# Retention, two feed-forward stages and a soft mixture on one Trainium2 core: loads into the packs' places queued behind the last turning transfers, sums of the last softmax stage in two banks, second expert layer begun on half of its inputs

## The chip, the cores and the metric

The program runs on one core of a Trainium2 chip. The metric is the device time of one execution in microseconds (us). The core has five engines: PE (TensorE; its weight loads stand in the profile as PEld), ACT (ScalarE), DVE (VectorE), POOL (GpSimd) and SP (SyncE). In this kernel SP computes nothing: it is the queue from which every transfer (DMA) is issued, in program order.

## The reference: what is computed

The reference, cut to what matters:

```python
scores = scale * q @ k.T                       # 8 batches, 8 heads, 576 positions, 64 columns
ret = scores * Dmat                            # gamma_h ** (i - j) for i >= j, else 0
x = (ret @ v) as 4608 tokens x 512
h = x @ w_in                                   # 512 x 2048
x = (h * sigmoid(1.702 * h)) @ w_out           # 2048 x 512
logits = x @ phi                               # 512 x 32: 8 experts of 4 slots
d = softmax of logits over the tokens          # all 4608
slot_input = d.T @ x                           # 32 slots x 512
for e in range(8):
    slot_out[e] = max(slot_input[e] @ w1[e], 0) @ w2[e]      # 512 x 1024, 1024 x 512
c = softmax of logits over the slots
out = c @ slot_out
```

The second mixture needs the softmax over all tokens, so its experts can begin only when the last token has been through everything before.

## The kernel before, in words

The 4608 tokens are worked on in 12 blocks of 384 (`NB`, `NBLK`). For each block, PE forms the product with `w_in` in 16 pieces of 128 columns (`expert_scores`, L345, tile `hp`), ACT applies the gate (`gelu`, L355, tile `gT`), and the result has to be turned from columns-by-tokens to tokens-by-columns. For all blocks but the last, DVE turns 32 x 32 squares (`turn_fc`, L374, tile `pre`) and 16 transfers for each half of a block put the squares into their places (`shuffle`, L382, tile `nat`). These 32 transfers of a block are called the turning transfers here. In the last block (`n = LAST = 11`) PE does the turning itself (L369, tile `tpg`). The attention of a block (lines 193 to 259) is woven in between the pieces of the block before it; its operands lie in the tiles called packs.

The product with `w_out` is put off: the slots are linear in it, so `slots_part` (L449, tile `Sg`) multiplies the block's softmax weights with the turned gate output `nat`, one block late. For block 10 this happens in the last block after the seventh piece (`LAST_SLOTS_AT = 6`), in 12 products that appear as 24 rows in a trace (two passes each). The first two of them read the half of `nat` that was put in place first, the next two the second half.

The tail (`tail`, from L551) begins after the sixteenth piece of block 11: last logits, last softmax, `Sg` of block 11 (L602), the turning of the sums `acc` (L627), the product of the sums with `w_out` (L634, `si_ps`, one bank of PSUM, read out half by ACT at L638 and half by DVE at L639), the sum over the four column groups (L642), the first expert layer (L657, `h_ps`: 8 experts x 2 halves of 512 hidden columns), its turning (L665 to L676: two copies `hs`, 8 products `hT_ps` into one bank, a maximum with 0 into the zeroed tiles `hT`), the second expert layer in four quarters `q` of the 512 output columns (`second_layer`, L685, `so_ps`; each quarter reads 8 weight tiles), and for each quarter the sum over column groups (`slot_results`, L695) and the combination with `cT` (`result`, L710), whose five pieces are copied by ACT and DVE into tiles `ob` (L711) and written out (L712). Pieces of quarter `q - 1` stand between the experts of quarter `q`.

**The loads.** The tail needs 72 weight tiles of 128 x 1024 numbers of 4 bytes (512 KB each): 8 of the joined `w_out`, 32 of `w1`, 32 of `w2`. They are issued in the fixed order `todo` by `prefetch` (L480 to L498). Each takes the next *place*: a tile whose earlier content is done with. The places become free in the order of the program: a part of a buffer called `ring` and the buffer `raw`, the two `pre` buffers (3 each), 8 tiles of a pool `pw2` over the memory of the attention's packs (L765 to L767, opened in block 10 after its fourteenth piece), 3 views of the block's `x` (L776), the sixteen `w_in` tiles one after the other as block 11 finishes with them (L788), 4 tiles `pw3` over the memory of the gate (L586 to L588; beside them the pool holds two `hT` tiles and `hs`, 3 more tiles of the same size), 5 tiles `pt` (L616 to L618), and from then on the places of tiles that have been used in the tail (8 at L652, 4 after each expert at L660).

A load waits on SP until its place is free, and everything behind it on SP waits too. Each transfer also waits until the transfer issued eight before it has landed, so that at most eight are under way. The output is written in 20 pieces from SP as well, behind the last load.

Queue in block 10 around the change, as the loop of L730 to L767 issues it: the first 16 turning transfers of the block (after its tenth piece), 3 loads into `pre` (after the twelfth), 8 loads into `pw2` (after the fourteenth), the last 16 turning transfers (after the sixteenth).

Of the kernel before, what the change touches and what calls it, by code (L numbers as in the profile page):

```python
# [20 lines left out]
DM = H * D  # L21
DFF = 2048
NS = 32
NE = 8
SE = 4
EF = 1024
# [7 lines left out]
NFC = DFF // 128  # L34
# [5 lines left out]
NW3, NW4 = 4, 5  # L40
NQ = 4
# [88 lines left out]
def tile_kernel(ctx, tc, qkv, w_in, w_turned, w_out, phi, w1, w2, consts, out):  # L130
# [346 lines left out]
    def place_in(pool_, tag, bufs):  # L477
        return lambda: pool_.tile([128, 1024], F32, tag=tag, name="wx", bufs=bufs)
# [72 lines left out]
    def tail():  # L551
# [15 lines left out]
        act.copy(Lp[0:NS, 1], lt[0:NS])  # L567
# [7 lines left out]
        dve.reduce_max(mb, lt, axis=AX.X)  # L575
        dve.tensor_tensor(mnew, mb, st["m"], op=ALU.max)
# [9 lines left out]
        pw3 = ctx.enter_context(tc.tile_pool(name="pw3", bufs=NW3, side="right", reuse_waits="tile"))  # L586
# [4 lines left out]
        for t in hT_flat:  # L591
            pool.memset(t, 0.0)
# [24 lines left out]
        for _ in range(NW4):  # L617
            prefetch(place_in(pt, "w", NW4))  # L618
        ST = pt.tile([128, 4, 4, NS], F32, tag="s", name="ST", bufs=2)
# [10 lines left out]
        si_ps = ps.tile([128, DM], F32, tag="r", name="si_ps", bufs=3)  # L630
        for fl in range(4):
            for b in range(4):
                fc = 4 * b + fl
                pe.matmul(si_ps[32 * b:32 * b + 32, :], ST[:, fl, b, :], wx[0, fc // 2][:, fc % 2, :],  # L634
                          start=(fl == 0), stop=(fl == 3))
        combine_rest(NPRE, NTILE)
        dve.transpose(cT, Lall)
        act.activation(si4[:, 0:256], si_ps[:, 0:256], AF.Copy, scale=ssum)  # L638
        dve.tensor_scalar(si4[:, 256:512], si_ps[:, 256:512], ssum, None, op0=ALU.mult)  # L639
        sit_ps = ps.tile([128, NDC, NS], F32, tag="L", name="sit_ps")  # L640
        for dc in range(NDC):
            pe.matmul(sit_ps[:, dc, :], si4[:, dc * 128:(dc + 1) * 128], sum4[:, 0:NS], start=True, stop=True)  # L642
# [7 lines left out]
        dve.tensor_copy(own_slots(si_flat, 0, NE, NDC), sit_ps.rearrange("p c (e j) -> p e c j", j=SE))  # L650
# [4 lines left out]
        for e, hf in [(e, hf) for e in range(NE - 2) for hf in range(2)] + [(e, hf) for hf in range(2) for e in (NE - 2, NE - 1)]:  # L655
# [4 lines left out]
            if hf and e < NE - 2:  # L660
                for _ in range(NDC):
                    prefetch()

        hT = [t.rearrange("p (e c s) -> p e c s", c=EF // 128, s=NS) for t in hT_flat]
        act.copy(hs[:, 0], h_ps[0])  # L665
        act.copy(hs[:, 1, 0:256], h_ps[1][:, 0:256])
        dve.tensor_copy(hs[:, 1, 256:512], h_ps[1][:, 256:512])
        hT_ps = ps.tile([128, EF // 128, NS], F32, tag="L", name="hT_ps")
        for f in range(EF // 128):
            pe.matmul(hT_ps[:, f, :], hs[:, f // 4, (f % 4) * 128:(f % 4 + 1) * 128], sum4[:, 0:NS], start=True, stop=True)  # L670
        hv = hT_ps.rearrange("p c (e j) -> p e c j", j=SE)
        for i, k in ((0, 0), (0, 4), (1, 0), (1, 4)):
            c = slice(k, k + 4)
            dve.tensor_scalar(own_slots(hT_flat[i], 16 * i, 3, EF // 128)[:, :, c], hv[:, 4 * i:4 * i + 3, c], 0.0, None,
                              op0=ALU.max)
            dve.tensor_scalar(hT[i][:, 3, c, 16 * i + 12:16 * i + 16], hv[:, 4 * i + 3, c], 0.0, None, op0=ALU.max)  # L676
# [3 lines left out]
        def second_layer(q, e):  # L680
            if e == 0:
                SR[q] = ps.tile([128, DQ], F32, tag=("St", "L")[q % 2], name="so_ps")
            for f in range(EF // 128):
# [15 lines left out]
        homes = [(pw3, NW3)] * NW3 + [(pt, NW4)] * NW4  # L699

        def result(q, k):

            nt = min(8, NTILE - 8 * k)
            own, m = homes.pop(0)
            homes.append((own, m))
            ob = own.tile([128, 1024], F32, tag="w", name="ob", bufs=m)[:, 0:128 * nt]
            ov = ob.rearrange("p (t b i) -> p t b i", b=4, i=32)
            for b in range(4):
                op_ = ps.tile([128, 8, 32], F32, tag=("h", "r")[b % 2], name="op", bufs=3)[:, 0:nt]
                pe.matmul(op_, SR[q][32 * b:32 * b + 32], cT[32 * b:32 * b + 32, 8 * k:8 * k + nt, :], start=True, stop=True)  # L710
                (act.copy if b % 2 == 0 else dve.tensor_copy)(ov[:, :, b, :], op_)  # L711
            sp.dma_start(out[q, :, 1024 * k:1024 * k + 128 * nt], ob)  # L712

        NG = (NTILE + 7) // 8
        for q in range(NQ):
# [8 lines left out]
        for k in range(NG):  # L724
            result(NQ - 1, k)
# [107 lines left out]
```

## Time and profile before

| | |
|---|---|
| median of 3 runs | 683.14 us (681.36 to 685.93) |
| the profiled execution's own time | 682.53 us |
| its span, first to last instruction | 680.7 us |
| PE busy | 647.0 us, 95% of the span |
| DVE, ACT, POOL busy | 44%, 32%, 12% |
| moved by transfers | 150.67 MB, 221 GB/s over the span |
| output transfers | 16 of 512 KB and 4 of 256 KB |

Rows of the timeline give the start in us from the span's start, the time, the engine, the source line and the operation; in brackets stands how long the engine was idle before and what ended it. A row can merge several instructions (`x20`). SPq is SP as a queue: its time is issue time, not the transfer's. In rows by stretch, each engine's busy time stands with its number of instructions, then the granted clock of TensorE as a share of 2.4 GHz, the mean busy share of the 16 DMA engines and what they moved.

### The profile page before, as it was taken

Reading aid. Unit: us, or ns where it says so; the run is one execution under the profiler, and the core shown is the slowest. Engines: PE = TensorE matmul, PEld = TensorE weight load, DVE = VectorE, ACT = ScalarE, POOL = GpSimd, SP = SyncE. Lnnn points to the kernel's source line nnn. Section 1 sums busy time; section 2 is a strip of 40 time slices with the busy share of each in tenths; the row PEclk is TensorE's granted clock in tenths of the full one; section 3 lists DMA queues with packets and bytes.
Section 4 is the critical chain, followed back from the end, with each engine's and each line's share of the span. In section 5 each row is a group of like instructions: output and inputs, shape, how many; then the busy total and the mean of one; then the engine's idle time right before and its main releaser. Section 6 shows DMA issues by size and latency. Waiting matters only on the chain.

```text
span 680.7 us, 19516 instructions
## 1 busy us (share of the span) xinstructions
PE 647.0 (95%) x8595; PEld 550.0 (81%) x8595; DVE 297.3 (44%) x594; ACT 220.6 (32%) x429; POOL 80.2 (12%) x72
## 2 busy tenths in 40 slices
PE   8699999899999999999999999999999996998994
PEld 8697788688997988989989979899899894863663
DVE  3799824334453462454444533534544331222143
ACT  1675332132241242232422412423324141230143
POOL 1102102111101102021011011111110000010000
PEclk9799999999999999999999999999999999999998
DMA  7989465586776747646747567476477388989998
GB/s 277 392 291 336 161 156 147 133 191 210 198 251 152 194 138 196 178 156 193 186 123 199 162 153 203 148 186 180 149 198 200 68 289 234 410 290 370 408 409 339
DMA packets 67732, 150.67 MB, mean 221 GB/s; under 512 B 8768, under 2 KB 42944, under 8 KB 63040
## 3 DMA queue, kind: packets, MB, share of 16 engines
q1 hardware_dynamic: 67648, 149.43, 69.6%
q8 instruction: 67, 1.10, 0.7%
q14 instruction: 17, 0.14, 0.1%
HBM read 101.16 MB, written 13.63 MB: 169 GB/s over the span
## 4 chain that ended last, share of the span: by engine, by line
PE 72%; DMA 16%; SPq 5%; DVE 4%; ACT 1%; issue 1%; ACTq 0%
PE hp L345 48%; DMA wx<-in_moe_w_dram 6%; PE Sg L449 5%; PE Lg L389 4%; SPq L382 4%; DMA pack<-in_qkv_dram 4%; PE Sp L216 4%; PE St L216 3%; PE Op L216 2%; DMA early_raw<-in_moe_w_in_dram 2%; DMA out_dram<-ob 2%; DMA nat<-pre 1%; PE op L710 1%; PE warm L515 1%; DMA wx<-wo_dram 1%
## 5 line engine op out<-in xcount | busy, mean ns | idle before, releaser
L345 PE MATMUL hp<-x,w 128*128 128x384 f32 x2304 | 423.9, 341 | 3.1 <-ACT x L241 2.6
L345 PEld LDWEIGHTS hp<-x,w 128*128 128x128 f32 x2304 | 399.4, 189 | 30.4 <-issue 21.5
L374 DVE STREAM_TRANSPOSE pre<-gT 128x384 f32<-128x384 f32 x172 | 96.9, 572 | 185.8 <-ACT gT L355 159.6
L355 ACT ACTIVATE gT<-hp 128x384 f32<-128x384 f32 x188 | 91.4, 489 | 235.2 <-PE hp L345 235.1
L246 POOL TENSOR_TENSOR x<-xs,x 128x512 fp32r<-128x512 f32 x33 | 42.7, 1293 | 301.4 <-ACT x L241 301.4
L216 PE MATMUL Op<-pack 64*64 64x64 f32 x2176 | 72.2, 220 | 3.0 <-issue 2.4
L216 PEld LDWEIGHTS Op<-pack 64*64 64x64 f32 x2176 | 66.8, 135 | 3.6 <-issue 2.8
L222 POOL TENSOR_TENSOR pack<-pack,cs 128x512 f32<-128x512 f32 x32 | 34.5, 1080 | 170.3 <-DMA pack<-in_qkv_dram 129.2
L241 ACT CAST x<-xs 128x512 fp32r<-128x512 f32 x36 | 22.3, 620 | 87.6 <-DVE xs L234 87.6
L216 PE MATMUL Sp<-pack 64*64 64x64 f32 x1152 | 41.1, 222 | 3.3 <-DMA pack<-in_qkv_dram 3.3
L216 PEld LDWEIGHTS Sp<-pack 64*64 64x64 f32 x1152 | 37.7, 138 | 4.9 <-issue 2.6
L216 PEld LDWEIGHTS St<-pack 64*64 64x64 f32 x1024 | 33.2, 137 | 8.1 <-issue 8.1
L389 PE MATMUL Lg<-gT,Wp 128*32 128x384 f32 x376 | 38.5, 496 | 1.2 <-DVE Wp L322 0.7
L449 PE MATMUL Sg<-nat,dn 128*32 128x512 f32 x264 | 33.8, 617 | 5.3 <-DMA nat<-pre 5.3
L226 DVE TENSOR_TENSOR pack<-Sp,cs 128x512 f32<-128x512 f32 x36 | 24.8, 689 | 30.7 <-PE Op L216 19.8
L216 PE MATMUL St<-pack 64*64 64x64 f32 x1024 | 37.5, 224 | 0.1
L449 PEld LDWEIGHTS Sg<-nat,dn 128*32 128x32 f32 x264 | 9.4, 113 | 24.7 <-issue 24.6
L234 DVE TENSOR_TENSOR xs<-Op,cs 128x512 f32<-128x512 f32 x36 | 24.5, 680 | 4.4 <-PE Op L216 4.4
L290 ACT ACTIVATE early_raw<-early_raw 128x512 f32<-128x512 f32 x28 | 19.2, 690 | 18.0 <-DMA early_raw<-in_w_turned_dram 9.1
L230 DVE TENSOR_TENSOR pack<-St,cs 128x512 f32<-128x512 f32 x32 | 21.7, 680 | 4.6 <-PE St L216 3.4
L455 DVE SCALAR_TENSOR_TENSOR acc<-acc,corr,Sg 128x512 f32<-128x512 f32 x10 | 7.5, 748 | 36.2 <-PE Sg L449 36.2
L711 DVE COPY ob<-op 128x256 f32<-128x256 f32 (+1 forms) x40 | 14.0, 393 | 21.1 <-PE op L710 16.4
(127 smaller groups left out, 390.7 us busy)
## 6 DMA issues: line engine op xcount, KB each, us to landing
pack<-in_qkv_dram SPq DMA_DIRECT2D x36, 1024.0 KB, 5.6
nat<-pre SPq DMA_DIRECT2D x352, 96.0 KB, 2.2
wx<-in_moe_w_dram SPq DMA_DIRECT2D x60, 512.0 KB, 8.6
raw<-in_moe_w_out_dram SPq DMA_DIRECT2D x16, 512.0 KB, 4.8
out_dram<-ob SPq DMA_DIRECT2D x16, 512.0 KB, 9.2
early_raw<-in_moe_w_in_dram SPq DMA_DIRECT2D x14, 512.0 KB, 9.6
early_raw<-in_w_turned_dram SPq DMA_DIRECT2D x14, 512.0 KB, 6.8
wo_dram<-ring SPq DMA_DIRECT2D x16, 256.0 KB, 2.0
```

The costliest lines, as they stand in the source:

```text
L216: pe.matmul(o[oh, p, j, :], w[h, a, p, j], w[h, b, p, j], start=first_, stop=True, skip_group_check=True)
L222: pool.tensor_tensor(k, k, by_state(ksc[:, n % NPB, :]), op=ALU.mult)
L226: dve.tensor_tensor(packs[n][:, SC], Sps.pop(n), across(dtab), op=ALU.mult)
L234: dve.tensor_tensor(xss[g], Ops.pop(g), across(osc), op=ALU.mult)
L241: act.copy(xh[b_][:, :, i * CP:(i + 1) * CP], xss[g].rearrange("p a j c -> p a (j c)"))
L246: (eng or pool).tensor_tensor(xl[b_][:, :, cols_], xss.pop(g).rearrange("p a j c -> p a (j c)"), xh[b_][:, :, cols_], op=ALU.subtract)
L345: pe.matmul(hp, wt[fc][:, a, dc, :], b[n][:, dc, :], start=(i == 0), stop=(i == 3 * NDC - 1))
L355: act.activation(gT[n, g][:, fl, :], hps.pop((n, fc)), AF.Gelu_apprx_sigmoid)
L374: dve.transpose(pre[n, hf][:, :, :, fh, :].rearrange("p c b i -> p (c b) i"), gT[n, g][:, fl, :].rearrange("p (x j) -> p x j", j=32))
L382: sp.dma_start(nat[n][32 * b:32 * b + 32, :, a, hf * HF:(hf + 1) * HF, :], pre[n, hf][32 * a:32 * a + 32, :, b])
L389: pe.matmul(Lg[n][32 * fl:32 * fl + 32, :], Wp[:, g * GF + fl, :], gT[n, g][:, fl, :], start=(g == 0), stop=(g == NFC // GF - 1))
L449: pe.matmul(Sg[32 * b:32 * b + 32], dn[n][:, c, :], nv[:, 4 * b:4 * b + 4], start=(c == 0), stop=(c == NT128 - 1))
```

## The change

It has six parts.

1. The 8 loads into `pw2` are issued after block 10's sixteenth piece and behind `shuffle(n, 1)`, the last turning transfers, instead of in front of them.
2. `pw3` holds 7 places instead of 4. `hT` (2 tiles) and `hs` have no memory of their own any more: they take the first three places that the first layer's first expert leaves, and are zeroed then (POOL).
3. In the tail, DVE's maximum over `lt` stands ahead of ACT's copy of `lt` into `Lp` (they read one bank).
4. `si_ps` becomes two tiles of 256 columns in two banks (32 products of 256 columns for 16 of 512), both read out by ACT; `sit_ps` becomes two tiles; DVE's transposition of `cT` moves behind the copies into `siT`.
5. `hT_ps` becomes two tiles, a bank for each half of the hidden columns. The first half is turned while the second half of the last expert is still being formed, and quarter 0 of the second layer runs over all experts on inner columns 0 to 3 first, then on 4 to 7, with the turning of the second half after its fourth expert.
6. `result` forms two pieces at once (a whole bank for each `op` tile), after the fourth and sixth expert and one after the eighth; the 12 places `ob` go round among 7 + 5 instead of 4 + 5.

```diff
-NW3, NW4 = 4, 5
+NW3, NW4 = 7, 5
...
-        act.copy(Lp[0:NS, 1], lt[0:NS])
...
         dve.reduce_max(mb, lt, axis=AX.X)
+        act.copy(Lp[0:NS, 1], lt[0:NS])
...
-        for _ in range(NW3):
-            prefetch(place_in(pw3, "w", NW3))
-        hT_flat = [pw3.tile([128, 1024], F32, tag=f"hT{i}", name="hT", bufs=1) for i in range(2)]
-        hs = pw3.tile([128, 2, 512], F32, tag="hs", name="hs", bufs=1)
+        homes = [(pw3, f"w{i}", 1) for i in range(NW3)]
+        for i in (3, 4, 5, 6, 0, 1, 2):
+            prefetch(place_in(*homes[i]))
...
+        si_ps = [ps.tile([128, DM // 2], F32, tag="r", name="si_ps", bufs=3) for _ in range(2)]
+        for hf in range(2):
+            for fl in range(4):
+                for b in range(4):
+                    fc = 4 * b + fl
+                    pe.matmul(si_ps[hf][32 * b:32 * b + 32, :], ST[:, fl, b, :],
+                              wx[0, fc // 2][:, fc % 2, 256 * hf:256 * hf + 256], start=(fl == 0), stop=(fl == 3))
+        act.activation(si4[:, 0:256], si_ps[0], AF.Copy, scale=ssum)
+        act.activation(si4[:, 256:512], si_ps[1], AF.Copy, scale=ssum)
...
+        def turn_sums(i):
+            for f in range(4):
+                pe.matmul(hT_ps[i][:, f, :], hs[:, i, f * 128:(f + 1) * 128], sum4[:, 0:NS], start=True, stop=True)
...
+        for e in range(NE - 2):
+            for hf in range(2):
+                first_layer(e, hf)
+            if e == 0:
+                hT_flat = [places.pop(0)() for _ in range(2)]
+                hT = [t.rearrange("p (e c s) -> p e c s", c=EF // 128, s=NS) for t in hT_flat]
+                hs = places.pop(0)().rearrange("p (a f) -> p a f", a=2)
+                for t in hT_flat:
+                    pool.memset(t, 0.0)
+            for _ in range(1 if e == 0 else NDC):
+                prefetch()
+        first_layer(NE - 2, 0)
+        first_layer(NE - 1, 0)
         act.copy(hs[:, 0], h_ps[0])
...
+        first_layer(NE - 2, 1)
+        turn_sums(0)
+        first_layer(NE - 1, 1)
+        act.copy(hs[:, 1], h_ps[1])
...
+        for e in range(NE):
+            second_layer(0, e, range(0, 4))
+            if e == 3:
+                turn_sums(1)
+        for e in range(NE):
+            second_layer(0, e, range(4, 8))
+        sums_out(0)
+        for q in range(1, NQ):
             for e in range(NE):
                 second_layer(q, e)
-                if q and e == 1:
+                if e == 1:
                     slot_results(q - 1)
-                elif q and e > 2:
-                    result(q - 1, e - 3)
+                elif e in (3, 5, 7):
+                    result(q - 1, {3: (0, 1), 5: (2, 3), 7: (4,)}[e])
...
                     if fc == WINDOWS[-1]:
                         att_ctx.close()
                         pw2 = ctx.enter_context(tc.tile_pool(name="pw2", bufs=NW2, side="right", reuse_waits="tile"))
+                    if fc == NFC - 1:
                         for _ in range(NW2):
                             prefetch(place_in(pw2, "w", NW2))
```

Line numbers in the rows that follow, marked with - and +, are those of the kernel before and of the changed kernel. On SP, from the first half of block 10's turning transfers (`nat<-pre`) to the last load of a weight tile (`wx`, `ring`):

```order
 L382 DMA nat<-pre 32x3x256 x16
-L497 DMA wx<-wo_dram 128x1024 x6
-L497 DMA wx<-in_moe_w_dram 128x1024 x5
+L497 DMA wx<-wo_dram 128x1024 x3
 L382 DMA nat<-pre 32x3x256 x16
-L497 DMA wx<-in_moe_w_dram 128x1024 x31
+L497 DMA wx<-wo_dram 128x1024 x3
+L497 DMA wx<-in_moe_w_dram 128x1024 x39
 L497 DMA ring<-in_moe_w_dram 128x1024
-L497 DMA wx<-in_moe_w_dram 128x1024 x24
+L497 DMA wx<-in_moe_w_dram 128x1024 x21
```

Eleven loads stood ahead of the second 16 turning transfers, and three do now; behind them stand 64 instead of 56. Behind the load into `ring`, the first whose place the product with `w_out` leaves, 21 remain instead of 24.

On PE, from the last experts of the first layer (`h_ps`) to the first sum of quarter 0 (`sr_ps`), before:

```order
L657 MATMUL h_ps<-ring,siT 32x512 x3
L657 MATMUL h_ps<-wx,siT 32x512 x5
L657 MATMUL h_ps<-ring,siT 32x512 x3
L657 MATMUL h_ps<-wx,siT 32x512 x2
L670 MATMUL hT_ps<-sum4r,hs 128x32 x8
L685 MATMUL so_ps<-wx,hT 32x128 x56
L685 MATMUL so_ps<-ring,hT 32x128 x8
L685 MATMUL so_ps<-wx,hT 32x128 x16
L695 MATMUL sr_ps<-so_7516,sum4r 128x128
```

and now (the tiles `hs` and `hT` lie in places and are called `wx` here):

```order
L660 MATMUL h_ps<-wx,siT 32x512 x5
L660 MATMUL h_ps<-ring,siT 32x512
L666 MATMUL hT_ps<-sum4r,wx 128x32 x4
L660 MATMUL h_ps<-ring,siT 32x512 x2
L660 MATMUL h_ps<-wx,siT 32x512 x2
L701 MATMUL so_ps<-wx 32x128 x16
L666 MATMUL hT_ps<-sum4r,wx 128x32 x4
L701 MATMUL so_ps<-wx 32x128 x64
L711 MATMUL sr_ps<-so_7535,sum4r 128x128
```

The eight turning products stood together behind the last expert; four of them stand inside it now and four inside the second layer's quarter 0.

## Rows read from the trace of the kernel before

**Rows 1.** The page's head and its row of busy time.

```profile
span 680.7 us, 19516 instructions
PE 647.0 (95%) x8595; PEld 550.0 (81%) x8595; DVE 297.3 (44%) x594; ACT 220.6 (32%) x429; POOL 80.2 (12%) x72
```

**Rows 2.** Busy time by stretch, the last 130 us, core 0.

```profile
557.00:568.20 11.20, 10.70 (x67) 9.75 (x66) 5.16 (x12) 6.42 (x11) 0.00 (x0) 1.00 1.03 346
568.20:576.50 8.30, 2.99 (x15) 1.25 (x18) 0.00 (x0) 0.49 (x1) 0.00 (x0) 0.93 0.67 154
576.50:600.00 23.50, 23.50 (x152) 19.08 (x145) 3.53 (x6) 5.10 (x12) 0.00 (x0) 0.95 1.02 405
600.00:620.00 20.00, 17.48 (x126) 9.97 (x124) 7.77 (x21) 6.88 (x16) 2.82 (x3) 1.00 0.82 273
620.00:676.00 56.00, 48.51 (x824) 28.68 (x824) 15.61 (x50) 14.87 (x50) 0.00 (x0) 0.98 1.03 411
676.00:680.70 4.70, 0.00 (x0) 0.00 (x0) 0.00 (x0) 0.00 (x0) 0.00 (x0) 0.50 0.35 140
```

**Rows 3.** Timeline of PE, 563 to 582 us.

```profile
564.95 4.45 PE L345 MATMUL hp<-x,w 128*128 128x384 f32 x24
569.33 1.05 PE L449 MATMUL Sg<-nat,dn 128*32 128x512 f32 x4
575.69 4.24 PE L449 MATMUL Sg<-nat,dn 128*32 128x512 f32 x20 [5.31 <-DMA nat<-pre]
```

**Rows 4.** Timeline of SP, 540 us to the end: every transfer issued.

```profile
539.82 6.45 SPq L382 DMA_DIRECT2D nat<-pre  x10
548.91 2.73 SPq L497 DMA_DIRECT2D wx<-wo_dram  x6
551.68 4.92 SPq L497 DMA_DIRECT2D wx<-in_moe_w_dram  x5
557.60 16.39 SPq L382 DMA_DIRECT2D nat<-pre  x16
574.09 41.16 SPq L497 DMA_DIRECT2D wx<-in_moe_w_dram  x31
616.42 0.33 SPq L497 DMA_DIRECT2D ring<-in_moe_w_dram  x1
618.14 28.81 SPq L497 DMA_DIRECT2D wx<-in_moe_w_dram  x24
647.91 25.51 SPq L712 DMA_DIRECT2D out_dram<-ob  x20
```

**Rows 5.** Waits of SP, 500 us to the end: waited for, us in total, times, longest.

```profile
SPq L497 <- PE tpg L369: 12.9, 6, 2.7
SPq L497 <- PE hp L345: 6.3, 3, 2.7
SPq L827 <- DMA out_dram<-ob: 6.2, 1, 6.2
```

**Rows 6.** The line of the loads, L497: its transfers' time from issue to landing.

```profile
DMA to landing us min/median/max: 4.0/8.2/11.4
```

**Rows 7.** Timeline of DVE, 549 to 556 us: the last turning of block 10.

```profile
552.13 0.58 DVE L374 STREAM_TRANSPOSE pre<-gT 128x384 f32<-128x384 f32 x1 [1.50 <-ACT gT L355]
```

**Rows 8.** Timeline of the tail: `Sg`, quarter 0 of the second layer, the last copies.

```profile
610.15 2.78 PE L602 MATMUL Sg<-nat,dn 128*32 128x512 f32 x24 [0.35 <-DVE dn L597]
...
636.55 3.27 PE L685 MATMUL so_ps<-wx,hT 128*32 128x128 f32 x112 [0.30 <-DVE hT L674]
...
668.53 3.77 DVE L711 COPY ob<-op 128x256 f32<-128x256 f32 x10 [1.74 <-ACT SR L697]
```

**Rows 9.** Busy time by stretch, two stretches of 4 us, core 0.

```profile
552.00:556.00 4.00, 4.00 (x27) 3.12 (x26) 1.14 (x2) 1.07 (x3) 0.00 (x0) 1.00 0.94 351
576.00:580.00 4.00, 4.00 (x21) 0.95 (x14) 0.04 (x1) 0.00 (x0) 0.00 (x0) 0.66 0.99 369
```

More of the change, by code (lines that the diff above doesn't have):

```diff
@@ L585, in tail @@
         gate_ctx.close()
-        pw3 = ctx.enter_context(tc.tile_pool(name="pw3", bufs=NW3, side="right", reuse_waits="tile"))
-        for _ in range(NW3):
-            prefetch(place_in(pw3, "w", NW3))
-        hT_flat = [pw3.tile([128, 1024], F32, tag=f"hT{i}", name="hT", bufs=1) for i in range(2)]
-        hs = pw3.tile([128, 2, 512], F32, tag="hs", name="hs", bufs=1)
-        for t in hT_flat:
-            pool.memset(t, 0.0)
+        pw3 = ctx.enter_context(tc.tile_pool(name="pw3", bufs=1, side="right", reuse_waits="tile"))
+        homes = [(pw3, f"w{i}", 1) for i in range(NW3)]
+        for i in (3, 4, 5, 6, 0, 1, 2):
+            prefetch(place_in(*homes[i]))
         dp = ps.tile([128, NT128, 128], F32, tag="L", name="dp")
@@ L618, in tail @@
             prefetch(place_in(pt, "w", NW4))
+        homes += [(pt, "w", NW4)] * NW4
         ST = pt.tile([128, 4, 4, NS], F32, tag="s", name="ST", bufs=2)
@@ L629, in tail @@
         dve.tensor_copy(ST[:, 2:4].rearrange("p f b s -> p f (b s)"), tps[1])
[L630 to L635, printed above, removed]
+        si_ps = [ps.tile([128, DM // 2], F32, tag="r", name="si_ps", bufs=3) for _ in range(2)]
[7 more added lines that the diff above has]
+        act.activation(si4[:, 256:512], si_ps[1], AF.Copy, scale=ssum)
         combine_rest(NPRE, NTILE)
[L637 to L640, printed above, removed]
+        sit_ps = [ps.tile([128, 2, NS], F32, tag=t, name="sit_ps") for t in ("L", "St")]
         for dc in range(NDC):
-            pe.matmul(sit_ps[:, dc, :], si4[:, dc * 128:(dc + 1) * 128], sum4[:, 0:NS], start=True, stop=True)
+            pe.matmul(sit_ps[dc // 2][:, dc % 2, :], si4[:, dc * 128:(dc + 1) * 128], sum4[:, 0:NS], start=True, stop=True)
         def own_slots(t, s0, ne, n):
@@ L649, in tail @@
         siT = si_flat[:, 0:NE * NDC * NS].rearrange("p (e c s) -> p e c s", e=NE, s=NS)
-        dve.tensor_copy(own_slots(si_flat, 0, NE, NDC), sit_ps.rearrange("p c (e j) -> p e c j", j=SE))
+        for i in range(2):
+            dve.tensor_copy(own_slots(si_flat, 0, NE, NDC)[:, :, 2 * i:2 * i + 2],
+                            sit_ps[i].rearrange("p c (e j) -> p e c j", j=SE))
+        dve.transpose(cT, Lall)
         for _ in range(NFC // 2):
@@ L654, in tail, with first_layer @@
         h_ps = [ps.tile([128, 512], F32, tag="r", name="h_ps", bufs=3) for _ in range(2)]
-        for e, hf in [(e, hf) for e in range(NE - 2) for hf in range(2)] + [(e, hf) for hf in range(2) for e in (NE - 2, NE - 1)]:
+        hT_ps = [ps.tile([128, 4, NS], F32, tag=t, name="hT_ps") for t in ("L", "St")]
+        def first_layer(e, hf):
             for dc in range(NDC):
@@ L659, in tail @@
                           start=(e == 0), stop=(e == NE - 1))
[L660 to L664, printed above, removed]
-        act.copy(hs[:, 0], h_ps[0])
[L666 to L676, printed above, removed]
-        SR = {}
[L680 to L683, printed above, removed]
+        def turn_sums(i):
+            for f in range(4):
+                pe.matmul(hT_ps[i][:, f, :], hs[:, i, f * 128:(f + 1) * 128], sum4[:, 0:NS], start=True, stop=True)
+            hv = hT_ps[i].rearrange("p c (e j) -> p e c j", j=SE)
+            c = slice(4 * i, 4 * i + 4)
+            for k in range(2):
+                dve.tensor_scalar(own_slots(hT_flat[k], 16 * k, 3, EF // 128)[:, :, c], hv[:, 4 * k:4 * k + 3], 0.0, None,
+                                  op0=ALU.max)
+                dve.tensor_scalar(hT[k][:, 3, c, 16 * k + 12:16 * k + 16], hv[:, 4 * k + 3], 0.0, None, op0=ALU.max)
@@ new lines, in tail, with second_layer @@
+        first_layer(NE - 2, 0)
+        first_layer(NE - 1, 0)
+        act.copy(hs[:, 0], h_ps[0])
+        first_layer(NE - 2, 1)
+        turn_sums(0)
+        first_layer(NE - 1, 1)
+        act.copy(hs[:, 1], h_ps[1])
+        SR = {}
+        def second_layer(q, e, fs=range(EF // 128)):
+            if q not in SR:
+                SR[q] = ps.tile([128, DQ], F32, tag="r" if q == 0 else ("St", "L")[q % 2], name="so_ps",
+                                bufs=3 if q == 0 else 1)
+            for f in fs:
@@ L697, in slot_results @@
             act.copy(SR[q], sr_ps)
[L699 to L707, printed above, removed]
-            for b in range(4):
[L709 to L712, printed above, removed]
@@ L714, in tail, with result @@
-        NG = (NTILE + 7) // 8
-        for q in range(NQ):
+        def result(q, ks):
+            ops, nts = [], [min(8, NTILE - 8 * k) for k in ks]
+            for b in range(4):
+                ops.append(ps.tile([128, 2, 8, 32], F32, tag=("h", "r")[b % 2], name="op", bufs=3))
+            for i, k in enumerate(ks):
+                for b in range(4):
+                    pe.matmul(ops[b][:, i, 0:nts[i]], SR[q][32 * b:32 * b + 32],
+                              cT[32 * b:32 * b + 32, 8 * k:8 * k + nts[i], :], start=True, stop=True)
+            for i, k in enumerate(ks):
+                home = homes.pop(0)
+                homes.append(home)
+                ob = home[0].tile([128, 1024], F32, tag=home[1], name="ob", bufs=home[2])[:, 0:128 * nts[i]]
+                ov = ob.rearrange("p (t b i) -> p t b i", b=4, i=32)
+                for b in range(4):
+                    (act.copy if b % 2 == 0 else dve.tensor_copy)(ov[:, :, b, :], ops[b][:, i, 0:nts[i]])
+                sp.dma_start(out[q, :, 1024 * k:1024 * k + 128 * nts[i]], ob)
@@ L722, in tail @@
             sums_out(q)
         slot_results(NQ - 1)
-        for k in range(NG):
-            result(NQ - 1, k)
+        for k in range((NTILE + 7) // 8):
+            result(NQ - 1, (k,))
     with tc.manual_schedule(engines={getattr(mybir.EngineType, e) for e in ("PE", "Activation", "DVE", "Pool", "SP")}):
```

## The prediction

> **What bounds the kernel now.** I read the page's head first: PE is busy 95% of the span [rows 1]. That share is an average over the twelve blocks and says little about the end, where the whole change lies. So I next read the busy time by stretch, from 557 us on [rows 2]. From 576.5 to 600 us PE has no idle time and the transfers run at 405 GB/s with the DMA engines full. From 600 to 620 us the DMA share falls to 0.82 at 273 GB/s and PE is busy for 17.48 of 20 us. From 620 to 676 us the transfers run at 411 GB/s, without a break, while PE is idle for 7.5 of 56 us. So over the last 60 us the 16 DMA engines are the bound: the end comes when the last byte is out. The timeline of SP says the same at its end: the last of 20 output transfers has been issued at 647.91 + 25.51 = 673.4 us, and SP then waits 6.2 us for them to land [rows 4, 5], so the last lands at 679.6 us. The last copy on DVE ends at 668.53 + 3.77 = 672.3 us [rows 8], 7.3 us before that.
>
> Then I looked for idle time ahead of this stretch. PE: in 568.2 to 576.5 us it is busy for 2.99 of 8.3 us [rows 2]. The timeline of PE gives the place: four rows of Sg of block 10, an idle time of 5.31 us that the turning transfers end, then the other 20 rows in 4.24 us [rows 3]. In the tail 24 such rows take 2.78 us [rows 8], so 20 would take 2.32; the missing 1.9 us is the clock. The granted clock over 576 to 580 us is 0.66 [rows 9], part of the stretch at 1.2 instead of 2.4 GHz, after an idle PE. The stall thus costs PE 5.3 + 1.9 = 7.2 us. Transfers: between 600 and 620 us they move 273 where 411 would go, 20 x (1 - 273/411) = 6.7 us lost. The waits of SP say why: loads wait on PE's products and turnings, nine times, 19.2 us together [rows 5]. The queue runs dry because PE gives places back too late.
>
> **Calibrating the sum.** A unit is 512 KB, 524,288 bytes; at 405 to 411 GB/s it takes 1.295 to 1.276, say 1.285 us. The fastest load lands 4.0 us after its issue [rows 6], 2.7 more than its own unit. From 574.09 us on there are 31 + 1 + 24 = 56 loads [rows 4] and the output's 16 + 4/2 = 18 units: 74 x 1.285 = 95.1 us. If the engines were never idle, the last would land at 574.1 + 2.7 + 95.1 = 671.9. It lands at 679.6. Of the 7.7 us, 6.7 are the dry time above; the other 1.0 I take as the emptying of the 16 engines at the end, which stays.
>
> **The moved loads (part 1).** Now three loads stand ahead of the last 16 turning transfers instead of eleven. These transfers need DVE's last turning, which ends at 552.13 + 0.58 = 552.7 us [rows 7]. SP issues one in 6.45/10 = 0.645 us when nothing holds it [rows 4], 10.3 us for 16, so the last is out at 563.0. The wait for the transfer eight places before should not bite: three loads issued from 548.9 are 3.9 us of transfer and so land at about 555.5, and the sixth turning transfer, the first to wait for one of them, comes at 556. Before, PE started 575.69 - (557.60 + 16.39) = 1.7 us after the last issue [rows 3, 4]; so the half is in place at about 564.7. PE asks for it at 569.33 + 1.05 = 570.4 [rows 3]: 5.7 us of margin. The 5.31 us and the slow clock go, and all of PE behind it comes 7.2 us earlier.
>
> The price is that eight loads come later. The first of the 64 behind the turning transfers is issued at 563.0. By 574.1, when the first of 56 was issued before, (574.1 - 563.0)/1.285 = 8.6 units have gone through, against the 8 that were put behind. The stream is 0.6 unit, 0.8 us, ahead. No PE instruction between 563 and 606 us reads a loaded tile, so the delay itself stops nothing.
>
> **Three more places (part 2).** Of the loads, 21 instead of 24 remain behind the ring place. Three units, 3.9 us of transfer, can be issued earlier, when the gate's memory is free. That alone makes no byte fewer; it is a cushion for the stretch in which the queue ran dry. The memory of hT and hs now becomes free only after expert 0 and is zeroed then. The zeroing is POOL's, and its first reader comes six experts later: nothing.
>
> **The sum.** With places 7.2 us earlier, against 6.7 us of dry time, and three units of cushion, the queue should not run dry. Then 563.0 + 2.7 + (64 + 18) x 1.285 + 1.0 = 563.0 + 2.7 + 105.4 + 1.0 = 672.1 us for the last landing, 7.5 before 679.6 (0.8 + 6.7). At 1.276 and 1.295 us a unit it would be 671.3 and 672.9, and if the 1.0 us is not there, 671.1: the gain lies between 6.7 and 8.5.
>
> **Parts 3 to 6, PE's own chain.** PE's idle time in 600 to 620 us is 2.5 us [rows 2], and that is the most that the earlier maximum, the two banks of si_ps and the split of sit_ps can win there. Against it, 16 more products, 32 rows, stand in si_ps: at least 0, as the columns stay the same, and at most 32 x 3.27/112 = 0.93 us, the rate of the 128-column rows [rows 8], which I take as near 0 since 256 columns are the work. Turning inside the last expert can win the 0.30 us ahead of so_ps [rows 8] and perhaps as much again. So PE's last copy ends between 672.3 - 7.2 - 3.1 = 662.0 and 672.3 - 7.2 + 0.9 = 666.0. The last piece then needs 4.0 us or a little more to land alone, at most 670.5, still ahead of 672.1. I put these four parts at 0: the DMA stream covers them. If that cover were gone they would be worth what was just bounded. Pieces in pairs on 12 places ask nothing of the end, because output transfers already queue behind loads.
>
> So the profiled 682.53 would become 675.0. The median of the runs shown, 683.14, is 0.6 above that execution; on its scale I forecast 683.1 - 7.5 = 675.6 us.
>
> **A rate that speaks against it.** The sum needs 105 us at over 400 GB/s without a break. The rows have that for 80 us [rows 2], but not always: 351 GB/s at 552 to 556 and 369 at 576 to 580, both when a run of loads starts [rows 9]. The Trainium skill (SBUF — State Buffer, section "Summary: rules for kernel authors") says to reckon with about 358 GB/s between HBM and SBUF. By that a unit would be 1.46 us and the forecast 14.7 us later, 690.3, a slower kernel. The 411 GB/s over 56 us speak against the rule here, so I keep 1.285 and let the slow rate be a rival.
>
> **Rivals.**
> - *The queue still runs dry in part.* The turning transfers stay late, held by the three loads ahead of them (behind eleven loads the 16 took 16.39 us [rows 4]; at that pace the half would be in place at 570.8, 0.4 us after PE asks), or PE loses time elsewhere, with its clock low again. If PE gains 4 us instead of 7.2, dry time of about 2.7 us stays and the gain is 4.8: 678.3. For it: SP holds everything in order. Against it: the margin of 5.7 us.
> - *The move does not remove the wait.* PE finds another late input at Sg, or waits as long elsewhere before the places are given back. Then only the 0.8 us of the stream stays: 682.3. Against it: the other input, the block's softmax weights, was ready, since the first four rows ran.
> - *Slower: the stream's rate.* Place: the 82 units from 563 us on. Before, 11 loads went out while PE still had products to do and a dry stretch followed, so a low rate at the start of a run cost nothing; now every unit counts at the end. Break-even is 7.5/82 = 0.09 us more a unit, 381 GB/s. At 369 the end is 11.2 us later than forecast: 686.8. At 351 it is 17.1 us later: 692.7. For it: the two rows at the start of runs. Against it: 405 and 411 in long runs.
>
> **How the numbers follow.** About 1% is what a measurement of this kernel can tell from no change; faster by that is below 676.3, slower above 690.0. Forecast 0.69, with a range of its own of 673.5 to 678.5: three quarters of it, 0.53, below 676.3, the rest, 0.16, within 1%. Dry in part 0.18, wait not removed 0.08, both within 1%. Slow rate 0.05, counted as slower. So faster 0.53, same 0.42, slower 0.05. The range of 8 in 10 reaches from 672.0, the best of the sum with a median 2 us low, to 682.0, which takes in the partly dry queue and leaves out most of the last two cases.
>
> **What would show it.** Right: no idle time of PE of over 1 us at Sg of block 10, its 24 rows in about 2.8 us, no fall of the granted clock at 575 us, over 400 GB/s in every stretch from 566 us to the end, and the last landing near 672. Wrong: SP waiting on PE for places with the DMA share under 0.95 between 590 and 615 us (dry in part), Sg still waiting for turning transfers, or a stream below 385 GB/s. If DMA is idle near the end and PE is not, PE's chain was the bound and parts 3 to 6 mattered.

## The result and the profile after

The changed kernel takes 673.56 us (median of 4 runs, 671.62 to 674.96); the kernel before, run beside it, 682.25 us. The ratio is 0.9884, 95% interval 0.9843 to 0.9926: faster by 0.7 to 1.6%. A second series gave 673.71 us and 0.9897 (0.9871 to 0.9923). The forecast was 675.6 us, a gain of 7.5; the ratio of the first series is worth 0.0116 x 682.25 = 7.9 us.

The profiled execution took 674.96 us. The page's head and its row of busy time (engine, us, share of the span, instructions), which answer [rows 1]:

```profile
span 673.2 us, 19573 instructions
PE 644.5 (96%) x8627; PEld 553.7 (82%) x8627; DVE 295.7 (44%) x593; ACT 220.9 (33%) x430; POOL 80.4 (12%) x72
```

The busy times hardly moved; the end of the program did. Busy time by stretch of the changed kernel (stretch, its length, PE, PEld, DVE, ACT, POOL, granted clock, DMA share, GB/s), beside [rows 2]:

```profile
557.00:566.00 9.00, 8.50 (x54) 7.55 (x53) 4.57 (x11) 5.22 (x9) 0.00 (x0) 1.00 0.80 194
566.00:576.50 10.50, 10.50 (x74) 8.18 (x73) 1.86 (x3) 2.32 (x5) 0.00 (x0) 1.00 1.00 396
576.50:600.00 23.50, 22.57 (x147) 19.07 (x145) 3.65 (x8) 8.54 (x18) 0.00 (x0) 1.00 1.03 409
600.00:620.00 20.00, 18.83 (x197) 8.60 (x199) 5.69 (x17) 2.58 (x8) 2.82 (x3) 1.00 1.03 408
620.00:668.00 48.00, 39.65 (x744) 28.52 (x734) 14.66 (x48) 14.78 (x50) 0.00 (x0) 0.92 1.03 410
```

Both holes are gone. Around 570 us PE had been busy for 2.99 of 8.3 us; now it is busy throughout, and the clock stays at 1.00, the level of 2.4 GHz. From 600 to 620 us the transfers moved 273 GB/s; now 408. PE's timeline says the same of block 10's `Sg` (start, length, operation, count), where [rows 3] had four rows, a wait of 5.31 us and twenty rows in 4.24:

```profile
564.21 4.45 PE L345 MATMUL hp<-x,w 128*128 128x384 f32 x24
568.59 2.78 PE L449 MATMUL Sg<-nat,dn 128*32 128x512 f32 x24
```

SP's timeline, every transfer issued from 548 us on, beside [rows 4]:

```profile
548.65 1.27 SPq L497 DMA_DIRECT2D wx<-wo_dram  x3
552.01 10.54 SPq L382 DMA_DIRECT2D nat<-pre  x16
562.66 1.48 SPq L497 DMA_DIRECT2D wx<-wo_dram  x3
564.19 46.37 SPq L497 DMA_DIRECT2D wx<-in_moe_w_dram  x39
611.59 0.33 SPq L497 DMA_DIRECT2D ring<-in_moe_w_dram  x1
612.86 25.95 SPq L497 DMA_DIRECT2D wx<-in_moe_w_dram  x21
639.77 24.33 SPq L731 DMA_DIRECT2D out_dram<-ob  x20
```

Four of its waits from 500 us on (waited for, us in total, times, longest), beside [rows 5]:

```profile
SPq L497 <- DMA wx<-in_moe_w_dram: 42.1, 47, 1.2
SPq L853 <- DMA out_dram<-ob: 8.0, 1, 8.0
SPq L497 <- PE tpg L369: 5.3, 3, 2.7
SPq L497 <- PE hp L345: 0.3, 1, 0.3
```

The turning transfers took 10.54 us instead of 16.39 to issue, and the last left SP 562.55 - 551.98 = 10.6 us after DVE's turning instead of 573.99 - 552.71 = 21.3. What had held them are two waits of the kernel before that [rows 5] does not list (same view, 500 us to the end):

```profile
SPq L382 <- DMA wx<-in_moe_w_dram: 5.1, 5, 2.3
SPq L382 <- DMA wx<-wo_dram: 2.2, 3, 0.9
```

The five last loads ahead of them were themselves being issued until 551.68 + 4.92 = 556.6 us [rows 4]. Then the first eight turning transfers waited for the loads issued eight places ahead of them, 7.3 us together; the changed kernel has no such wait. Beside loads they were also slower to land. Time from issue to landing of the sixteen, before and then in the changed kernel:

```profile
DMA to landing us min/median/max: 2.2/6.0/10.8
DMA to landing us min/median/max: 2.2/2.7/3.5
```

Of the loads' waits for PE in [rows 5], 5.6 us in four are left of 19.2 us in nine; with the others, which neither list shows, 7.2 us in nine are left of 25.3 us in fifteen. The long row is their wait for transfers eight places earlier, which is what a full queue looks like from SP. The last output has been issued at 639.77 + 24.33 = 664.1 us, and 8.0 us later, at 672.1, the last has landed: the same 672.1 that was forecast.

That agreement is partly luck, and it needs a measure that is not. DVE's last turning of block 10, which releases the turning transfers, belongs to code that is the same in every kernel here; yet it ended anywhere between 547.9 and 553.9 us. So from here on each kernel is judged by its remainder, the time from the end of this turning to the landing of the last output, read in one profiled execution of each. Before, by [rows 7] and [rows 4, 5], it is 679.6 - 552.7 = 126.9 us. The turning in the changed kernel's DVE timeline:

```profile
551.40 0.58 DVE L374 STREAM_TRANSPOSE pre<-gT 128x384 f32<-128x384 f32 x1 [1.50 <-ACT gT L355]
```

It ends at 551.98, so the remainder is 120.1 us. Of the 7.5 us by which the two spans differ, 6.8 come from the changed stretch and 0.7 from ahead of it. In the second series the remainder was 120.5: half a microsecond of it says nothing.

### The profile page after: what moved, and what is told of

Same layout as the page of the kernel before. It is cut to its first block, busy times and chain, and to the rows that moved or that the text cites. A ratio compares the mean times of both kernels' runs of the same rounds, so it can differ in the third digit from the quotient of the medians.

```text
span 673.2 us, 19573 instructions
## 1 busy us (share of the span) xinstructions
PE 644.5 (96%) x8627; PEld 553.7 (82%) x8627; DVE 295.7 (44%) x593; ACT 220.9 (33%) x430; POOL 80.4 (12%) x72
## 3 DMA queue, kind: packets, MB, share of 16 engines
q8 instruction: 68, 1.11, 0.7%
## 4 chain that ended last, share of the span: by engine, by line
PE 83%; DMA 7%; DVE 4%; SPq 2%; ACT 2%; issue 1%; ACTq 0%
PE hp L345 52%; PE Lg L389 5%; PE Sg L449 4%; PE Sp L216 4%; DMA pack<-in_qkv_dram 4%; PE St L216 3%; PE so_ps L701 3%; PE Op L216 2%; PE h_ps L660 2%; PE op L722 2%; SPq L382 2%; DMA early_raw<-in_moe_w_in_dram 2%; PE warm L515 1%; DVE w L309 1%; PE tpg L369 1%
## 5 line engine op out<-in xcount | busy, mean ns | idle before, releaser
L355 ACT ACTIVATE gT<-hp 128x384 f32<-128x384 f32 x188 | 91.5, 490 | 234.0 <-PE hp L345 233.8
L449 PE MATMUL Sg<-nat,dn 128*32 128x512 f32 x264 | 31.6, 593 | 0.0
L290 ACT ACTIVATE early_raw<-early_raw 128x512 f32<-128x512 f32 x28 | 19.2, 689 | 17.1 <-DMA early_raw<-in_w_turned_dram 10.5
```

What stands on the lines that cost most here:

```text
L355: act.activation(gT[n, g][:, fl, :], hps.pop((n, fc)), AF.Gelu_apprx_sigmoid)
L449: pe.matmul(Sg[32 * b:32 * b + 32], dn[n][:, c, :], nv[:, 4 * b:4 * b + 4], start=(c == 0), stop=(c == NT128 - 1))
```

## The experiments

The theory on record, S, was that the end is set by a stream of loads and outputs that must start behind the turning transfers and never run dry. Rival P held that the three further places are needed for that, rival C that PE's own chain (parts 3 to 6) gives the gain, rival U that PE's lateness would not matter by itself. The table lists the kernels and what they took. Each ratio is to the kernel before, run beside it in the same series, where its median was 680.6 to 682.3 us; medians of different series should not be subtracted. The last copy is timed from the same turning to the end of the last copy into an output tile.

| kernel | median us | ratio (95%) | remainder us | last copy us |
|---|---|---|---|---|
| before | 682.25 | 1 | 126.9 | 119.6 |
| changed | 673.56 | 0.9884 (0.9843 to 0.9926) | 120.1 | 111.5 |
| changed, again | 673.71 | 0.9897 (0.9871 to 0.9923) | 120.5 | 111.2 |
| e1 order alone | 673.50 | 0.9881 (0.9854 to 0.9908) | 121.1 | 112.6 |
| e2 all but the order | 679.95 | 0.9978 (0.9956 to 0.9999) | 126.5 | 118.3 |
| e3 order and places | 674.08 | 0.9894 (0.9871 to 0.9916) | 119.8 | 111.5 |
| e4 all but places | 674.21 | 0.9910 (0.9884 to 0.9937) | 120.1 | 111.6 |
| e5 two pieces unwritten | 671.01 | 0.9846 (0.9816 to 0.9876) | 118.1 | 111.0 |
| e6 extra products | 675.02 | 0.9905 (0.9873 to 0.9937) | 121.8 | 117.5 |
| e7 two queues | 678.70 | 0.9960 (0.9932 to 0.9987) | 123.6 | 117.6 |
| e8 four among | 674.92 | 0.9917 (0.9886 to 0.9948) | 122.0 | 115.1 |
| e10 two ahead | 674.18 | 0.9903 (0.9877 to 0.9929) | 119.9 | 111.0 |
| e11 PE later | 678.58 | 0.9972 (0.9956 to 0.9989) | 126.2 | 119.4 |

**Which part gives the gain.** e1 is the kernel before with part 1 alone:

```
+                    if fc == NFC - 1:
                         for _ in range(NW2):
                             prefetch(place_in(pw2, "w", NW2))
```

> The kernel before with part 1 alone: the eight loads stand behind the last turning transfers, nothing else. Theory S (the end is set by a stream of transfers that is never idle once PE gives places back 7.2 us earlier): the whole gain, 7.5 us less than the kernel before, 0.989 of it, DMA share over 1.0 from 566 us to the end, no wait of PE for turning transfers. Rival P (the three more places carry the stream over the gap): the queue runs dry for part of the time, some 3.6 us less than before, 0.995. Rival C (PE's chain in the tail, parts 3 to 6, gives 2 to 3 us of it): some 5 us less, 0.993.

It gives the gain to within 1 us: the ratio is that of the changed kernel, the remainder 0.6 to 1.0 us above its two values. Busy time by stretch in e1:

```profile
576.50:600.00 23.50, 22.77 (x149) 19.34 (x141) 4.18 (x9) 8.87 (x20) 1.84 (x2) 1.00 1.03 409
600.00:620.00 20.00, 17.80 (x155) 6.12 (x159) 5.56 (x16) 1.72 (x5) 0.98 (x1) 1.00 1.03 408
```

The stream is as full as in the changed kernel, with 24 loads behind the ring load and PE's chain as before. P (0.995) and C (0.993) lie outside the interval and fall. e2 is the other half: the changed kernel without that `if`.

> The changed kernel with part 1 undone: the eight loads stand ahead of the last turning transfers again, parts 2 to 6 as changed. Theory S: PE waits 5.3 us for the turning transfers and runs at the lower clock after it, the queue runs dry between 600 and 620 us, and the time is 0 to 2 us under the kernel before, 0.997 to 1.0. Rival P: three more loads go out before the gap, 3.9 us less than before, 0.994. Rival C: 2 to 3 us less, 0.996.

The wait is back. PE's timeline in e2, and under it the stretches from 576.5 us:

```profile
566.89 1.05 PE L449 MATMUL Sg<-nat,dn 128*32 128x512 f32 x4
573.04 5.05 PE L449 MATMUL Sg<-nat,dn 128*32 128x512 f32 x20 [5.10 <-DMA nat<-pre]
```

```profile
576.50:600.00 23.50, 23.50 (x151) 20.24 (x146) 3.54 (x6) 5.51 (x12) 0.00 (x0) 0.98 0.96 378
600.00:620.00 20.00, 17.90 (x169) 10.14 (x171) 7.68 (x22) 6.97 (x16) 1.46 (x2) 1.00 0.91 331
```

So parts 2 to 6 without part 1 are worth 0.2%. Beside 409 GB/s, the rate of a full stretch, the two stretches lack 23.5 x (1 - 378/409) + 20 x (1 - 331/409) = 5.6 us of transfer, where those of [rows 2] lack 6.9: the dry stretch begins earlier and is a little softer, and the remainder falls by 0.4 us, which is within the scatter. With part 1 in place, e3 (parts 1 and 2) and e4 (all but 2) ask what the others add:

```
-NW3, NW4 = 4, 5      # e3: the kernel before with parts 1 and 2
+NW3, NW4 = 7, 5
...
-NW3, NW4 = 7, 5      # e4: the changed kernel, hT and hs with tiles of their own
+NW3, NW4 = 4, 5
```

> The kernel before with parts 1 and 2 (order and seven places), the tail's operations as before. Theory S: 7.5 us less than before, as with part 1 alone, 0.989. Rival P: 7.5 us less here, and clearly more than with part 1 alone. Rival C: 5 us less, 0.993, and the changed kernel's DMA share under 1.0 where PE is late.

> The changed kernel without part 2: four places, own tiles for hT and hs, nine places for the output pieces. Theory S: 7.5 to 8 us less than before, as the changed kernel, 0.988 to 0.989; 24 loads behind the one into ring, still with the DMA share over 1.0 throughout. Rival P: 3.6 us less, 0.995. Rival C: as theory S.

Nothing that can be measured, either way: the remainder is 119.8 and 120.1 us.

**Is it the stream?** e5 leaves two of the output's twenty transfers unwritten, whole pieces of 512 KB and so two of the forecast's units:

```
+            if q == 0 and k < 2:
+                continue
             sp.dma_start(out[q, :, 1024 * k:1024 * k + 128 * nts[i]], ob)
```

> The changed kernel, which leaves out two of the twenty output transfers (pieces 0 and 1 of quarter 0, 512 KB each). No computing instruction is left out. Theory S: two units fewer in the stream, 2 x 1.285 = 2.6 us less than the changed kernel, 0.9847 of the kernel before. Rival C: no change, 0.9885.

The remainder falls by 2.0 us (2.4 from the changed kernel's second value) where two units are 2.6. Bytes off the stream come off the end. e6 puts eight products ahead of the last quarter's results, work for PE that moves no byte:

```
+        for _ in range(8):
+            pe.matmul(spare[0:32], siT[:, 0, 0, :], wx[2, 3, 0].rearrange("p c d -> p (c d)")[:, 0:512], start=True, stop=True)
         slot_results(NQ - 1)
```

> The changed kernel with eight products of 512 columns more on PE (result unused) after the last quarter of the second layer, ahead of its sum: about 3.4 us more on PE at 2.4 GHz, up to 7 at 1.2. Theory S: PE's last copy has about 3 us in hand before the last transfers would be late, so 0 to 1 us more than the changed kernel at the upper clock, 0.9885 to 0.990 of the kernel before (up to 4 us more if the clock is low there). Rival C: 3.4 us more, 0.9935, at the upper clock.

The products came as 16 rows of 0.44 us, 7.05 us in all at a granted clock of 1.00, twice what was expected. The last copy ended 6.1 us later and the last landing only 1.7: PE's chain has about 6.1 - 1.7 = 4.4 us of slack at the end. The forecast had 672.1 - 670.5 = 1.6 us at the least. So parts 3 to 6 had cover.

**Is PE's lateness the cause of the dry stretch?** e11 delays PE ahead of block 10's sums in the changed kernel, with the transfers in time and the clock up:

```
             if fc == LAST_SLOTS_AT:
+                for _ in range(10):
+                    pe.matmul(spare[0:32], phis[:, 0, :], Wp.rearrange("p f s -> p (f s)"), start=True, stop=True)
                 slots_part(n - 1)
```

> The changed kernel with ten products of 512 columns more on PE (result unused) ahead of Sg of block 10, 4.3 us at 2.4 GHz. Theory S, as the prediction put it (each microsecond that PE comes later than 6.7 of its 7.2 us is one of dry queue): places come 4.3 us later, the queue runs dry for 3 to 4 us between 590 and 612 us, 3 to 4 us more than the changed kernel from DVE's last turning to the last transfer, 0.994 of the kernel before. Rival U (the eight transfers under way and the three more places are cushion enough): 0 to 1 us more, DMA share over 1.0 throughout.

The delay is larger than meant: 20 rows, 8.3 us for the 19 in the row below; the profile lists the last among the first rows of `Sg`. `Sg` begins 24.3 us after DVE's turning instead of 16.6. The added rows in PE's timeline, the two stretches, and SP's waits on PE in e11:

```profile
564.53 8.34 PE L811 MATMUL spare<-Wp,phis 128*32 128x512 f32 x19
```

```profile
576.50:600.00 23.50, 23.50 (x152) 21.59 (x151) 3.00 (x6) 5.88 (x13) 0.00 (x0) 1.00 0.93 364
600.00:620.00 20.00, 17.89 (x177) 8.73 (x179) 7.68 (x22) 6.47 (x15) 2.82 (x3) 1.00 0.93 350
```

```profile
SPq L497 <- PE tpg L369: 13.5, 6, 2.7
SPq L497 <- PE hp L345: 6.3, 3, 2.7
```

These waits on PE are back to 19.8 us in nine, as in [rows 5], and the stream runs dry: the two stretches lack 5.5 us of transfer beside 409 GB/s. The remainder grows by 6.1 of the 7.7 us, to 126.2, nearly that of before; by the medians of one series e11 is 678.58 - 673.71 = 4.9 us slower than the changed kernel. No load or turning transfer was touched. Nor is it PE's chain that ended last: in e11 the last landing comes 6.8 us after the last copy, and in e6 4.3 us between the two were enough. U falls: what the wait at `Sg` cost, it cost through the places that PE gave back late. What did not come back of the 7.7 us, 1.6 us by the remainder and 2.8 by the medians, is the room that PE has there.

**Can the turning transfers go out faster?** e7 issues every second one of the second half from ACT:

```
-sp.dma_start(nat...)
+(act if two and b % 2 else sp).dma_start(nat...)
```

> The changed kernel with every second of the last 16 turning transfers issued from ACT instead of SP. Theory S: SP is through with its eight in some 5 us, so the 64 loads begin about 5 us earlier; part of that is lost since they share the engines with ACT's eight, so 1.5 to 4 us less than the changed kernel, 0.983 to 0.986 of the kernel before. Against it: ACT issues for some 5 us and does no gates, so PE may stand still for up to 3 us in the first pieces of block 11; if that is given on to the places, no gain or 1 to 2 us more.

A miss: the remainder is 3.5 us longer than the changed kernel's. ACT's timeline (the issues, and the gate that comes behind them), PE's wait, and the stretch from 600 us:

```profile
552.41 7.88 ACTq L382 DMA_DIRECT2D nat<-pre  x8
560.39 0.49 ACT L355 ACTIVATE gT<-hp 128x384 f32<-128x384 f32 x1 [8.63 <-DMA nat<-pre]
```

```profile
561.90 1.01 PE L402 MATMUL lt<-Lp,sum4r 128*128 128x384 f32 x2 [5.51 <-DVE Lp L396]
```

```profile
600.00:620.00 20.00, 17.89 (x169) 10.34 (x171) 7.69 (x22) 6.99 (x16) 1.11 (x2) 1.00 0.91 335
```

ACT spends about 1 us on each issue and does no gates meanwhile; PE then waits 5.51 us for the softmax and begins `Sg` 23.2 us after DVE's turning instead of 16.6, its places come late, and the stream falls to 335 GB/s from 600 to 620 us. The first load behind the turning transfers came 7.6 us after DVE's turning instead of 10.7. The Trainium skill (DMA: Bandwidth & Descriptors, section "Rules for kernel authors") says that spreading transfers over issuing engines brings no bandwidth and saves sequencer time alone. The trace goes with the second half: the sixteen took 7.9 us to issue instead of 10.5, the time of ACT's eight, and it adds that this time was taken from ACT's own work. Whether the bytes moved any faster no run here shows.

**Is there room beside the turning transfers?** In the changed kernel the DMA engines look idle in part beside the turning transfers:

```profile
556.00:560.00 4.00, 4.00 (x24) 4.00 (x24) 2.03 (x6) 3.92 (x7) 0.00 (x0) 1.00 0.77 168
```

The share is 0.77. e8 sends four of the eight loads among the sixteen, one behind the second of every four:

```
+                    if b == 1:
+                        prefetch(among)
...
-                        for _ in range(NW2):
+                        for _ in range(NW2 - 4):
```

> The changed kernel with four of the eight moved loads issued among the last 16 turning transfers (one after the second of each four), the other four behind them. While the 16 are issued the DMA share is about 0.77, so there is room. Theory S: 60 loads instead of 64 remain behind them, their issue begins some 1.8 us later, so the stream ends 4 x 1.285 - 1.8 = 3.3 us earlier than in the changed kernel: 0.984 of the kernel before. The turning transfers are in place some 2 to 3 us later, inside the margin of 5.4 us, so PE does not wait. Rival C (PE's chain sets the end): as the changed kernel, 0.9885. Rival D (the turning transfers are late again): PE waits up to 2 us at Sg, the time is that of the changed kernel or up to 2 us longer.

A miss too: the remainder is 1.9 us longer. SP's timeline (the first and the last of the turning transfers, with the first load behind them), the stretches of e8, the turning transfers' time to landing, and PE at `Sg`:

```profile
549.04 1.23 SPq L382 DMA_DIRECT2D nat<-pre  x2
...
562.23 2.32 SPq L382 DMA_DIRECT2D nat<-pre  x2
564.60 1.54 SPq L499 DMA_DIRECT2D wx<-in_moe_w_dram  x3
```

```profile
552.00:556.00 4.00, 4.00 (x24) 4.00 (x24) 1.10 (x5) 2.90 (x6) 0.00 (x0) 1.00 1.06 244
556.00:560.00 4.00, 3.96 (x24) 3.61 (x23) 3.77 (x7) 2.78 (x4) 0.00 (x0) 1.00 1.06 227
```

```profile
DMA to landing us min/median/max: 5.1/5.9/6.8
```

```profile
565.62 1.05 PE L451 MATMUL Sg<-nat,dn 128*32 128x512 f32 x4
569.80 2.77 PE L451 MATMUL Sg<-nat,dn 128*32 128x512 f32 x20 [3.13 <-DMA nat<-pre]
```

The share is full at 227 to 244 GB/s. Sixteen transfers and four loads took 549.04 to 564.55, 15.5 us instead of 10.5: the four loads cost 5.0 us, what they bring (4 x 1.285 = 5.1). The expectation let them cost 1.8, so 3.3 us of them had to fit into idle time; yet the idle share that it read off was worth 0.23 x 10.5 = 2.4 us at the most. And the half is late again: a turning transfer took 5.9 us to land (median) instead of 2.7, and PE waits 3.13 us at `Sg`. The stream still did not run dry, at a share of 1.01 and 400 GB/s from 600 to 620 us; where the 1.9 us went was not found out. e10 puts two loads ahead of the sixteen instead:

> The changed kernel with two of the eight moved loads ahead of the last 16 turning transfers (five in all, instead of three) and six behind them. Theory S: the sixth to eighth turning transfer wait for loads issued eight before, the 16 end some 1.6 us later, 62 loads instead of 64 remain: 2 x 1.285 - 1.6 = 1.0 us less than the changed kernel, read in the trace from DVE's last turning of block 10 to the last transfer (119.8 us in the changed kernel), and no wait of PE at Sg. Theory M (a turning transfer beside loads costs the engines as much as the load brings, as with four among them): no gain, 0 to 1 us more.

The sixteen took 12.37 us, 1.8 more, and PE did not wait. The remainder is 119.9: 0.2 to 0.6 us less than the changed kernel's two values where 1.0 was expected. That is within the scatter; whether two loads ahead help is open. Beside it ran the changed kernel again, for the second series told above (the 119.8 us that two of the expectations give for its remainder are the 120.1 of the table):

> The changed kernel unaltered, beside the other two on the same chip. Theory S and all rivals: 0.9885 of the kernel before within the interval; 119.8 us from DVE's last turning of block 10 to the last transfer within 0.7 us, if the scatter of the times lies ahead of that point.

No kernel here that writes the whole output was measurably faster than the changed one; e1, a single line away from the kernel before, is as fast within the scatter.

## Why the prediction was right

**What bounds the kernel** was read rightly: the DMA stream of the last 110 us (e5, e6), with a dry stretch that PE's late places made (e11).

**The sum.** From the first load behind the turning transfers to the last landing 2.7 + 105.4 + 1.0 = 109.1 us were forecast; it took 672.1 - 562.66 = 109.4. The larger part of what was off lies in the turning transfers: the first load behind them came 562.66 - 551.98 = 10.7 us behind the turning instead of 10.3. Together 0.7 us, the difference between the forecast 7.5 and the 6.8 in the remainder. That the profiled end fell on 672.1 all the same is the 0.7 us that this execution was ahead before the change began.

**Part 1.** The wait at `Sg` and the low clock went as said. From the first row of `Sg` to the last it had been 579.93 - 569.33 = 10.60 us [rows 3] and is 2.78: 7.8 us, against 7.2 forecast. The forecast left out the four rows before the wait, and it put all 1.9 us that the twenty lost down to the clock. In e8 the same rows stand in two pieces at a granted clock of 1.00, and take 1.05 and 2.77 us where 24 in one piece take 2.78. So 1.05 + 2.77 - 2.78 = 1.0 us is the price of the break itself, and the clock cost 4.24 - 2.77 = 1.5; with the wait that is 5.3 + 1.0 + 1.5 = 7.8.

**Part 2, the cushion,** is not needed: e4 has none and loses nothing. The forecast counted it only as a reason why the queue should not run dry; PE's earlier places were enough. e11 shows how narrow that is: 1.6 to 2.8 us.

**Parts 3 to 6 at nothing:** right, and the cover that was named hid them. What they do inside it came out mixed. In the changed kernel's timeline:

```profile
599.73 0.37 PE L580 MATMUL dr<-ident,Lp 32*128 32x32 f32 x3 [0.93 <-ACT Lp L575]
601.58 2.78 PE L599 MATMUL Sg<-nat,dn 128*32 128x512 f32 x24 [0.35 <-DVE dn L594]
...
610.82 11.30 PE L660 MATMUL h_ps<-wx,siT 128*32 128x512 f32 x99
...
632.95 0.64 PE L701 MATMUL so_ps<-wx 128*32 128x128 f32 x14 [1.40 <-issue]
...
658.03 5.10 PE L722 MATMUL op<-cT,SR 32*128 32x256 f32 x40 [0.35 <-ACT SR L713]
```

The earlier maximum only moves the wait: PE now waits 0.93 us for ACT's copy, and `Sg` begins 49.6 us after DVE's turning in the changed kernel as in e3. The first layer begins 58.8 us after it instead of 59.9, in both series, so part 4 wins 1.0 us. Not all of it lasts to the last products, which begin 106.05 us after the turning (106.6 in the second series) instead of 106.9: ahead of `so_ps`, for one, PE stands still for 1.40 us (1.67 in the second series, 1.11 in e3) without a releaser that the profile names. Here the last products then take 5.10 us, since the granted clock is at the level of 1.2 GHz from 660 us on; PE had been busy for 3.00 of the 4 us before:

```profile
656.00:660.00 4.00, 3.00 (x34) 2.17 (x32) 1.94 (x7) 1.92 (x9) 0.00 (x0) 0.99 1.03 414
660.00:664.00 4.00, 3.13 (x24) 2.81 (x19) 2.61 (x7) 2.27 (x7) 0.00 (x0) 0.50 1.03 413
```

In e3 they take 4.27 us, and the last copy ends at 111.5 us in both. But that fall of the clock belongs to this execution and not to the change. The same kernel in the second series (its last products, and the 4 us in which they begin):

```profile
656.07 4.27 PE L722 MATMUL op<-cT,SR 32*128 32x256 f32 x40 [0.35 <-ACT SR L713]
```

```profile
656.00:660.00 4.00, 3.91 (x39) 3.35 (x40) 2.86 (x8) 2.75 (x10) 0.00 (x0) 1.00 1.04 418
```

e10 too had PE busy for 3.00 of 4 us there, and its clock stayed at 1.00. Why it fell in one execution is open; the last landing is the stream's in any case.

**The slow rate** did not come. The stream ran at 409, 408 and 410 GB/s over 91.5 us, and at 396 in the 10.5 us at the start of the run, where the forecast feared 351 to 369; its sign of being right, over 400 from 566 us on, was missed there by 4. The 358 GB/s that the Trainium skill says to reckon with (SBUF — State Buffer, section "Summary: rules for kernel authors") do not hold here. The Trainium skill has the other figure as well (HBM Reference, section "Specifications (TRN2)"): a core that streams alone reaches about 425, and the smaller one is its share when both cores of a pair stream. The rates here lie between the two figures, near the upper; a run with both cores streaming was not made.

**The other rivals** had the right mechanisms in the wrong kernel: "runs dry in part" is what e7 and e11 show, whose remainders are 3.5 and 6.1 us longer than the changed kernel's.

## What to carry to other kernels

An engine's wait off the final path costs what the resource behind it goes without: ask what becomes free late, and look for the stretch, here 30 us later, in which a queue runs dry for it. Where one queue carries both urgent transfers and a long stream, see that the urgent ones are in time, and ask what the stream loses meanwhile; here three loads ahead of them, or five (e10), did no harm, while eleven (before), or three and four among them (e8), made PE wait. Compare kernels from a common point just ahead of the change when what lies before it scatters by as much as the change is worth.

## What was not expected of the hardware

A DMA share of 0.77 beside turning transfers was no room for four loads: with loads put among them the share went to 1.06 at 227 to 244 GB/s, where loads alone run at 408 to 410. The turning transfers were slower too: 2.7 us from issue to landing (median) in the changed kernel, 4.4 with two more loads ahead (e10), 5.9 with four among them (e8), 6.0 behind eleven (before). What makes the two slower together was not found out.

The added products were each two rows of 0.44 us (8.34/19 in e11), where `Sg`'s rows of the same shape take 2.78/24 = 0.12. `Sg` goes round the four groups of 32 output rows; the added ones all went to one.
